# Loading the first two x tiles already transposed, and the KV transposes one Q unit later

## The chip, the cores and the metric

The kernel runs on one NeuronCore of one Trainium2 chip. The metric is the device time of one execution in microseconds (us). A profile records one execution; its span runs from the first to the last instruction that the profiler shows. Engines are named as in the profile: PE is TensorE's matmul, PEld its weight load, DVE is VectorE, ACT is ScalarE, POOL is GpSimd, SP is SyncE, which here issues DMAs only.

## The reference: what is computed

For x of 2048 tokens by 1024 features, in bf16:

```python
g = sigmoid((x * gate_w).sum(-1))
# A: linear attention, 32 heads of 32
q, k, v = split(x @ wqkv)
phi(t) = where(t > 0, t + 1, exp(t)) + 1e-6
kv = sum_s phi(k)^T v ;  z = sum_s phi(k)
o = (phi(q) @ kv) / (phi(q) @ z + 1e-6)
a = o @ wo
# B: one token, chosen by a router, goes through a gated FFN
r = x @ w_r ;  idx = argmax(r)
y = (silu(x[idx] @ w_gate) * (x[idx] @ w_up)) @ w_down
b = x ;  b[idx] += sigmoid(r[idx]) * y
out = g * a + (1 - g) * b
```

## The kernel before

The sequence is cut into 16 tiles of 128 tokens, the features into 8 chunks of 128. TensorE wants x with features on the partitions, so a transposed copy `xT` (128 x 8 chunks x 2048) is kept on chip. The work comes in three stages:

1. Keys and values. For each tile, `kv_mm` multiplies the tile of `xT` (as weights) with the key columns of wqkv, two halves of 512 columns, 8 chunks each; `unit_V` does the same for the value columns, and for the router's and gate's vectors, which stand in two further columns of `wkv`. ACT and DVE apply phi. `unit_KVACC` adds up phi(k)^T v and the sum of phi(k) of a tile in one bank, `kvacc`. The FFN of the one token is woven in on DVE and TensorE.
2. Queries. `unit_Q(g, j)` makes 128 query features for 512 tokens in 8 products (`ps` from `xT` and `wq`), and ACT and DVE turn them into `pq_all`. Most of them are woven into stage 1; the last ones come after it. Among these last ones stand the FFN's final sum (`down_finish`, tile `yps`), the denominators (`den_group`, tile `dps`), the transposition of kv (`unit_kvT`, tile `pt`, 32 products on tiles of 32 x 32 of the array), and the product of kv with wo (`unit_M`, tile `pm`), which reads `kvT`.
3. Output. For each tile, 16 products of `pq_all` with that merged matrix `m_sb`, then a mix with x by the gate, and a store.

The order on each engine is that of the program where the flag `strict` is set: the helper `in_order` (line 78) then chains each instruction of an engine behind the one before it. All of them are recorded under its line, 83, so groups are told apart by their tiles. Where `strict` is off, a scheduler orders by data dependence.

The start of the kernel matters here. TensorE begins with `N_WARM` = 6 products of constants (`warm`, lines 263 to 267, tile `warm_ps`). Meanwhile SP issues on its one queue, in this order (lines 136 to 150): x tile 0, key chunk 0 (`load_k(0)`, called k0 below), x tile 1, key chunks 1 to 7 (k1 to k7), the last 10 heads of the values (called v), then DMA transposes that write `xT` directly (tiles 2 and 3 one by one, then three groups of four tiles), the rest of the values, and `wq`. Tiles 0 and 1 come as they lie in memory (`xnat`); `unit_T` (line 200) transposes such a tile on TensorE, 8 blocks of 128 x 128 into two banks (`pst`), which DVE and ACT copy to `xT`. Then the first two tiles' key products run side by side, so that each chunk of the keys serves 4 products as it arrives: `first_mm(t, c0, c1)` (line 272) does 2 products of 512 columns per tile and chunk, into four banks called `first`. Tile 0's chunk c goes together with tile 1's chunk c - 1. The small product `wps` (line 281) puts the router's and gate's vectors into `wkv`.

PSUM has 8 banks: `ps_work` 4, `ps_ffn` 1, and 3 that are first `ps_t`, then `ps_acc` and `ps_red`, then `ps_den`.

The order at the end of the queries is given by these lines:

```python
    down_finish()
...
    rdA = den_group(0)
    strict[0] = True
    unit_kvT()
    strict[0] = False
    normalise(rdA, 0)
    normalise(rdA, 1)
    strict[0] = True
    for i in range(len(q_units)):
        unit_Q(*q_units.popleft())
        if i in M_AFTER:
            unit_M(*M_AFTER[i])
```

## Time and profile before

| what | us |
|---|---|
| three executions | 248.56, 248.9, 249.45 |
| median | 248.9 |
| the profiled execution | 248.56 |
| its span | 247.0 |
| PE busy | 240.8 (97% of the span) |
| DVE busy | 172.7 (70%) |
| ACT busy | 127.6 (52%) |
| POOL busy | 52.5 (21%) |
| TensorE clock granted, mean | 1.000 |

The profile has a page and a trace behind it. The chain that ended last is followed back from the last instruction: at each step to what released it, or to the instruction before it on its engine; in order of time it shows what the end of the kernel depended on. A timeline gives start, length, engine, line, operation, the tile written and the tile read; `x8` merges eight instructions. For a DMA two times are given: how long its issue kept SP (SPq), and how long it took from the start of its issue until its data had landed. A table by stretch gives, for stretches of the span, each engine's busy time, the granted clock, the share of the DMA engines' time in use, and what they moved in GB/s.

### The profile page before, as it was taken

Reading aid. Unit: us, or ns where it says so; the run is one execution under the profiler, and the core shown is the slowest. Engines: PE = TensorE matmul, PEld = TensorE weight load, DVE = VectorE, ACT = ScalarE, POOL = GpSimd, SP = SyncE. Lnnn points to the kernel's source line nnn. Section 1 sums busy time; section 2 is a strip of 40 time slices with the busy share of each in tenths; the row PEclk is TensorE's granted clock in tenths of the full one; section 3 lists DMA queues with packets and bytes.
Section 4 is the critical chain, followed back from the end, with each engine's and each line's share of the span. In section 5 each row is a group of like instructions: output and inputs, shape, how many; then the busy total and the mean of one; then the engine's idle time right before and its main releaser. Section 6 shows DMA issues by size and latency. Waiting matters only on the chain.

```text
span 247.0 us, 4867 instructions
## 1 busy us (share of the span) xinstructions
PE 240.8 (97%) x1898; PEld 123.6 (50%) x1923; DVE 172.7 (70%) x264; ACT 127.6 (52%) x215; POOL 52.5 (21%) x100
## 2 busy tenths in 40 slices
PE   8999999999999999999999999999999999999994
PEld 3466756654554554554554555544443444444442
DVE  0053124379984989845989999996789999954342
ACT  3195343355566376545555555668887633333300
POOL 6000000400000100000003300101666689950000
PEclk9999999999999999999999999999999999999999
DMA  6999995499969993599699690000004754464122
GB/s 207 343 239 195 267 392 151 108 326 337 281 194 292 341 290 88 149 312 384 224 345 340 230 280 3 3 4 21 0 3 127 204 182 148 155 190 166 48 82 86
DMA packets 46311, 47.78 MB, mean 193 GB/s; under 512 B 16776, under 2 KB 35472, under 8 KB 46224
## 3 DMA queue, kind: packets, MB, share of 16 engines
q1 hardware_dynamic: 45648, 46.28, 61.5%
q0 software_dynamic: 608, 1.19, 1.7%
q8 instruction: 15, 0.25, 0.5%
q14 instruction: 8, 0.07, 0.1%
q10 hardware_dynamic: 32, 0.00, 0.0%
HBM read 39.33 MB, written 8.39 MB: 193 GB/s over the span
## 4 chain that ended last, share of the span: by engine, by line
PE 97%; issue 1%; DVE 0%; DVEq 0%
PE ps L83 88%; PE first L83 3%; PE kvacc L83 2%; PE warm_ps L83 1%; PE red L83 1%; PE dps L83 1%; PE pst L83 1%; PE pm L83 1%; DVE ot L83 0%; PE yps L83 0%; PE pt L83 0%; DVEq L739 0%; PE hps L83 0%; PE rps L83 0%; PE wps L83 0%
## 5 line engine op out<-in xcount | busy, mean ns | idle before, releaser
L83 PE MATMUL ps<-wkv,xT 128*128 128x352 bf16 (+2 forms) x600 | 106.1, 334 | 0.4
L83 PEld LDWEIGHTS <-xT 128*128 128x128 bf16 x640 | 62.1, 98 | 49.1 <-issue 0.3
L83 ACT ACTIVATE u<-ps 128x512 f32<-128x512 f32 x60 | 35.9, 598 | 46.3 <-PE ps L83 45.7
L83 PE MATMUL ps<-xT,wq 128*128 128x512 bf16 x245 | 57.3, 379 | 0.6 <-issue 0.2
L83 PE MATMUL ps<-m_sb,pq_all 128*128 128x512 bf16 (+2 forms) x259 | 55.4, 373 | 0.3
L83 ACT ACTIVATE e<-u 128x512 f32<-128x512 f32 x64 | 40.3, 630 | 2.0
L83 PEld LDWEIGHTS <-pq_all 128*128 128x128 bf16 x264 | 25.4, 98 | 30.2 <-issue 0.7
L641 POOL TENSOR_TENSOR pq_all<-pq_all,rb 128x512 bf16<-128x512 bf16 x32 | 36.4, 1171 | 12.1 <-DVE rb L83 11.5
L83 PEld LDWEIGHTS <-wq 128*128 128x128 bf16 x256 | 24.5, 98 | 28.2 <-issue 1.0
L83 DVE SCALAR_TENSOR_TENSOR gacc<-wt,hcol,gacc 128x1024 f32<-128x1024 bf16 x27 | 34.5, 1278 | 0.4
L83 DVE SCALAR_TENSOR_TENSOR ot<-ps,gate,xg 128x512 bf16<-128x512 f32 (+2 forms) x33 | 23.9, 738 | 14.3 <-PE ps L83 13.1
L83 DVE SCALAR_TENSOR_TENSOR gacc<-wt,xs_f,gacc 128x2048 f32<-128x2048 bf16 x14 | 32.8, 2345 | 0.2
L83 ACT ACTIVATE xg<-xt,omg 128x1024 f32<-128x1024 bf16 x16 | 18.2, 1147 | 26.8 <-DVE ot L83 25.8
L83 DVE SCALAR_TENSOR_TENSOR pq_all<-ps,e 128x512 bf16<-128x512 f32 x32 | 21.9, 687 | 11.3 <-ACT e L83 11.3
L83 DVE SCALAR_TENSOR_TENSOR pk<-ps,e 128x512 bf16<-128x512 f32 x28 | 19.0, 686 | 11.8 <-ACT e L83 11.6
L83 DVE STREAM_SHUFFLE rb<-rdp 128x512 f32<-128x512 f32 x32 | 22.8, 753 | 0.0
L83 ACT CAST vt<-ps 128x352 bf16<-128x352 f32 x32 | 14.4, 453 | 11.4 <-PE ps L83 11.1
L214 POOL MEMSET vt<- 128x22 bf16 x16 | 3.7, 432 | 75.7 <-PE kvacc L83 75.2
L83 ACT CAST vc<-ps 128x320 bf16<-128x320 f32 x16 | 6.5, 428 | 7.3 <-PE ps L83 7.3
L83 DVE COPY rg<-ps 128x2 f32<-128x2 f32 x16 | 2.5, 159 | 10.2 <-ACT vc L83 10.1
L355 POOL DMA_DIRECT2D xs<-in_A_x_dram x1 | 0.7, 711 | 39.3 <-DVE sig L83 39.3
L83 DVE SCALAR_TENSOR_TENSOR pk<-first,e 128x512 bf16<-128x512 f32 x4 | 2.8, 692 | 7.9 <-ACT e L83 7.9
(100 smaller groups left out, 94.9 us busy)
## 6 DMA issues: line engine op xcount, KB each, us to landing
wt<-in_B_w_down_dram SPq DMA_DIRECT2D x14, 512.0 KB, 4.9
wt<-in_B_w_gate_dram SPq DMA_DIRECT2D x8, 512.0 KB, 7.6
wt<-in_B_w_up_dram SPq DMA_DIRECT2D x8, 512.0 KB, 8.3
xt<-xp SPq DMA_DIRECT2D x16, 256.0 KB, 2.7
out_dram<-ot SPq DMA_DIRECT2D x15, 256.0 KB, 2.0
wt<-in_B_w_gate_dram SPq DMA_DIRECT2D x8, 384.0 KB, 7.6
wt<-in_B_w_up_dram SPq DMA_DIRECT2D x8, 384.0 KB, 7.2
wkv<-in_A_wqkv_dram SPq DMA_DIRECT2D x8, 256.0 KB, 4.4
```

The lines of the kernel that those rows point to most:

```text
L83: inst = fn(*a, **k)
L214: nc.gpsimd.memset(vt_t[t][:, :, 32:33], 1.0)
L355: nc.gpsimd.dma_start(out=xs8[:], in_=x2d[bass.ds(idx_val, 1), :].rearrange("o (c p) -> (o c) p", p=P))
L641: nc.gpsimd.tensor_tensor(sl, sl, rb[:], op=ALU.mult)
```

## The change

Tiles 0 and 1 of x are no longer loaded as they lie and transposed on TensorE. SP issues a DMA transpose for each of them, at the places of the queue where the plain loads stood. `unit_T` and its calls go, with three short warm-up products; the long warm-ups become 8, and two short ones stand behind `wps`, which takes a bank of `ps_t` in place of that of `ps_ffn`. On the other side, `yps` takes the bank of `ps_ffn` and `dps` one of `ps_den` in place of banks of `ps_work`, and `unit_kvT` stands behind the first Q unit that follows the denominators, not in front of it.

```diff
-N_WARM = 6
+N_WARM = 8
...
-    def load_x(t0, n):
-        xt4 = xin.tile([P, n, D], BF, name=f"xnat{t0}", bufs=1)
-        sp.dma_start(out=xt4[:, 0:n, :], in_=x_v[:, t0 : t0 + n, :])
...
-    load_x(0, 1)
+    def load_xt(t):
+        sp.dma_start_transpose(out=xT[:, :, t * P : (t + 1) * P], in_=x2d[t * P : (t + 1) * P, :])
+
+    load_xt(0)
     load_k(0)
-    load_x(1, 1)
+    load_xt(1)
     for c in range(1, KC):
         load_k(c)
...
-    unit_T(0)
-    warm(3, 128)
     first_mm(0, 0, 1)
-    wps = ps_ffn.tile([P, 16], BF, tag="f")
+    wps = ps_t.tile([P, 16], BF, tag="t")
     pe.transpose(wps[:], wrg_rows[:], ident[0:16, 0:16])
     dve.tensor_copy(wkv[:, :, 2 * D : 2 * D + 2], wps[:].rearrange("p (w c) -> p c w", w=2))
-    unit_T(1)
+    warm(2, 128)
...
     def down_finish():
-        ps = ps_work.tile([P, 512], F32, tag="w", name="yps")[:, 0:256]
+        ps = ps_ffn.tile([P, 256], F32, tag="f", name="yps")
...
     def den_group(pair):
-        pool, tag = (ps_work, "w") if pair == 0 else (ps_den, "d")
-        dps = pool.tile([P, 512], F32, tag=tag, name="dps")
+        dps = ps_den.tile([P, 512], F32, tag="d")
...
     rdA = den_group(0)
-    strict[0] = True
-    unit_kvT()
-    strict[0] = False
...
     for i in range(len(q_units)):
         unit_Q(*q_units.popleft())
+        if i == 0:
+            unit_kvT()
         if i in M_AFTER:
             unit_M(*M_AFTER[i])
```

## The prediction

> **What bounds the kernel now.** I read the page's busy shares and its chain that ended last, then the same chain in order of time for the first 14 us, then the SP queue's issues one by one with their landings, then the DMA rate by stretch. The shares and the chain's summary on the page:

> ```profile
> PE 240.8 (97%) x1898; PEld 123.6 (50%) x1923; DVE 172.7 (70%) x264; ACT 127.6 (52%) x215; POOL 52.5 (21%) x100
> ...
> PE 97%; issue 1%; DVE 0%; DVEq 0%
> ```

> TensorE's work is the time: whatever delays it by 1 us costs 1 us, and removed work pays only where TensorE would otherwise have had data. The chain in order of time (start, length, what):

> ```profile
> 1.02 2.72 PE warm_ps L83 x6
> 3.74 1.02 PE pst L83 x8
> 4.76 0.32 PE warm_ps L83 x3
> 5.08 0.85 PE first L83 x2
> 5.93 0.12 PE wps L83
> 6.05 0.59 PE pst L83 x8
> 6.64 4.59 PE first L83 x21
> ...
> 162.25 0.31 PE pt L83 x32
> ```

> Two things are to be seen. The x transposes (pst, 1.02 and 0.59 us) stand before 6.64. And TensorE is slow at first: a 512-column product takes 0.85/2 = 0.43 us at 5.08 (a warm-up 2.72/6 = 0.45) and 4.59/21 = 0.22 from 6.64. So it ran at half speed until about 6.1 us, after some 5.1 us of unbroken work.

> What are the transposes in front of? Timeline of SP, and issues with landings (last number: us from issue to landing), asked for one at a time: the issue of key chunk 1 (k1), the first two DMA transposes, the landing of k1.

> ```profile
> 2.39 0.43 SPq L83 DMA_DIRECT2D wkv<-in_A_wqkv_dram  x1
> ```
> ```profile
> 6.51 4.36 SPq L83 DMA_TRANSPOSE xT<-in_A_x_dram  x1
> ```
> ```profile
> 10.92 1.75 SPq L83 DMA_TRANSPOSE xT<-in_A_x_dram  x1
> ```
> ```profile
> wkv<-in_A_wqkv_dram SPq DMA_DIRECT2D x1, 256.0 KB, 4.1
> ```

> k1 lands at 2.39 + 4.1 = 6.49, and the products that read it start at 6.64. From there TensorE needs 4 x 0.219 = 0.87 us per chunk and runs dense to 13.17; the last chunk, k7, issued at 5.24 with 5.7 to its landing, is there at 10.94 for a product at about 11.9. So the pst work lies almost wholly in the wait for k1: only 6.64 - 6.49 = 0.15 us of it is on the path. Later pieces of the same queue are as tight: the v part lands at 5.71 + 7.2 = 12.91 for 13.17, the first large transpose at 12.72 + 7.9 = 20.62 for a product at 20.98.

> DMA rate by stretch (last column GB/s; the first is the stretch in us):

> ```profile
> 2.70:6.50 3.80, 3.80 (x25) 2.01 (x24) 0.65 (x3) 1.07 (x2) 2.23 (x16) 1.00 0.98 334
> 6.50:11.20 4.70, 4.70 (x24) 2.11 (x23) 0.38 (x1) 0.58 (x1) 0.00 (x0) 1.00 1.05 359
> 12.00:12.75 0.75, 0.75 (x5) 0.32 (x4) 0.00 (x0) 0.60 (x1) 0.00 (x0) 1.00 1.00 111
> 12.75:14.00 1.25, 1.25 (x10) 0.82 (x9) 0.58 (x1) 1.21 (x3) 0.00 (x0) 1.00 1.28 288
> 14.00:15.20 1.20, 1.20 (x11) 0.85 (x10) 0.75 (x2) 1.17 (x3) 0.00 (x0) 1.00 0.81 126
> 27.75:29.00 1.25, 1.25 (x11) 0.90 (x10) 0.16 (x1) 0.58 (x2) 0.00 (x0) 1.00 0.99 80
> ```

> Copies run at 334 to 359, a transpose at best at 288. Where the queue passes from copies to transposes (12.00) it drops to 111, at the start of a large transpose (14.00) to 126, from transposes back to copies (27.75) to 80.

> **Part one: the x tiles.** *Removed:* 16 transposes (1.02 + 0.59 us of chain), 3 short warm-ups (0.32), two copies of 0.42 us on DVE and two of 0.59 on ACT. On the path they are worth 0.15 us, as above; next late is k1. *Added, hidden:* two warm-ups of 0.45, so the eight end at 1.02 + 8 x 0.453 = 4.64; the cover is the first product's wait for k0, which lands no earlier than its 4.24 of now (1.44 + 2.8). Without it they would cost 0.4. Two short warm-ups (0.21) lie in the wait for k1.

> *Moved:* SP issues transpose 0, k0, transpose 1, k1 to k7, v, then all it issued before. What stands behind the two transposes is every key chunk, the v part, transposes of tiles 2 to 15, and wq; TensorE waits for all of them in turn. An issue of x took 0.40 and 0.45 us. An issue of a transpose of the same 128 rows took 4.36 and 1.75. The 4.36 I read as a full queue: counting issued packets less those done in the trace, some 1,500 to 1,700 were outstanding at the end of every one of the five transposes' issues, long or short, so the issue waits for room; at 1 us the queue is empty. I therefore take the nearest row, 1.75, for both: k0 is issued at 0.98 + 1.75 + 0.05 = 2.78, and lands 2.8 later at 5.6; transpose 1 is issued at 3.2, k1 at 5.04 and lands, with x0's own 2.7 from issue to landing on a short queue, at 7.74. The chunk-1 products start there and not at 6.64: **+1.1 us**. Later pieces come at their old spacing behind k1, so they add nothing of their own.

> Bounds of this term by the stream. Rate alone: two times 0.262 MB at 288 in place of 345 GB/s is 0.15 us each, k1 at 6.79, +0.15. All switches charged: two passes from transpose to copy (1.25 us at 80 of 383 loses 0.99), one from copy to transpose (0.75 us at 111 of 288 loses 0.46), one slow start (1.2 us at 126 of 282 loses 0.66), and the rate: 3.4 us, k1 at 9.9, +3.25. The issue row lies between.

> [...]

> **The clock.** Now TensorE works without a gap from 1.02. After, it idles from 4.64 to 5.6 and, after two products, wps and two warm-ups (0.85 + 0.12 + 0.21), from 6.8 to 7.74. What such gaps do is not in the trace. At best nothing. At worst the 5.1 us of slow work start afresh with k1, and half of it is lost: 2.55. Before k1 there are 3.62 + 1.18 = 4.8 us of work, nearly the 5.1 that sufficed, so I take a value near the lower end: **+0.5**. [...]

> **Part two: kvT, yps, dps.** The same 32 + 8 + 16 products, other banks. kvT (pt, 0.31) moves behind one unit of 8 Q products. TensorE passes once more from small tiles to whole ones; after such a passage 32 products took 169.57 - 162.56 = 7.01 us, where 16 took 3.40 without, so one costs 0 to 7.01 - 6.80 = 0.21: **+0.1**. Waits it could add are covered: pt needs the dps bank back from ACT (0.69 us from 162.4) and the yps bank from DVE (0.48 from 161.7), both during that Q unit (1.73). DVE's kvT copies stand behind the 3.35 us reciprocal as now, and end near 167.4 for a first reader (pm) at 169.6; without that cover pm and all products behind it would slip one for one. Q units get their four banks back; no bank wait over 0.2 us stands in the chain there, so I book no gain.

> **Sum.** Against the profiled execution (248.56, span 247.0): 248.56 + 1.1 + 0.5 + 0.1 = 250.26. The median of the three runs, 248.9, is 0.34 above it; with that, **250.6**.

> **Rivals.** (a) *The transposes come like copies* (lower bounds; the queue is empty, and the 1.75 too was waiting for room): k1 by 6.8 to 7.3, clock as now, 248.56 + 0.15 to 0.75, with the 0.34 up to 249.6: no change. (b) *The switches and the clock*: for it, 80 GB/s for 1.25 us; against, that was before chunks of other shape. k1 at 8.5 to 9.9, and longer gaps leave the clock low: +1.9 to 3.25, +0.1, +0.6 to 2.55: 251.5 to 254.4. A one-time cost of the first transpose (4.36 - 1.75 = 2.6 us) would land here too. (c) *Faster*: the copies' slow beginning (193 GB/s from 2.0 to 2.7) is spared and k1 lands early. With 288 there, 0.45 us; with the 0.15 of removed transposes 0.6; it decides only if k1 lands before 5.9, and v and the large transpose (0.26 and 0.36 us of room) must come earlier too. 247.9 to 248.1. That the change does not do what it says cannot be: in the built order no x transpose is left on TensorE.

> **Numbers.** 0.3% (0.75 us) is about what a measurement can tell from no change. Forecast (249.65 to 251.5): 0.47; (a) 0.22; (b) 0.25; (c) 0.06. Faster 0.06, same 0.22, slower 0.72. Range from the lower bound, 248.7, to all upper bounds at once, 248.56 + 3.25 + 2.55 + 0.1 = 254.4.

> **What would show it.** Issue of the first transpose near 1.75 us (0.4: (a); over 4: one-time cost); k1 landed near 7.7 and the chunk-1 products starting there; those products 0.43 us long (clock) or 0.22; the products from 13 us on as dense as now; pt 8 products behind dps with no wait in front of pm. I am wrong if k1 lands by 6.8, or if the delay at the front is made up by a wait that vanishes later.

## The result and the profile after

The changed kernel takes **255.08 us** (median of 4 runs, 254.47 to 255.52) against 248.84 for the kernel before, measured beside it on the same chip (4 runs, 248.56 to 249.45): a ratio of 1.0246, 95% interval 1.0214 to 1.0277. The forecast of 250.6 had the direction and missed the size; its range ended at 254.4. The profiled execution took 255.52, with a span of 254.0, so it is 6.96 longer than the profiled one of before.

Busy shares and the chain's summary on the page of the changed kernel:

```profile
PE 242.5 (95%) x1884; PEld 123.1 (48%) x1908; DVE 171.9 (68%) x262; ACT 126.6 (50%) x213; POOL 52.6 (21%) x100
...
PE 94%; DMA 2%; SPq 1%; issue 1%; DVE 0%; DVEq 0%
```

TensorE is still the time, but with 15 products fewer it is busy 1.7 us longer, and the chain now holds DMA and SP's queue beside it. Where, the chain in order of time tells (start, length, what):

```profile
0.98 1.36 SPq L83
...
3.02 1.24 SPq L83
...
4.31 5.22 DMA wkv<-in_A_wqkv_dram
...
9.57 9.23 PE first L83 x30
...
90.42 0.32 PE ps L83
90.75 1.12 issue
91.86 9.68 PE ps L83 x49
...
169.12 1.83 PE ps L83 x8
170.95 0.22 PE pt L83 x32
```

Read from the top: SP issues transpose 0 (1.36 us), k0, transpose 1 (1.24 us), and k1 at 4.31, 1.92 later than before. k1 takes 5.22 to its landing, where it took 4.1. The products of chunk 1 start at 9.57 and not at 6.64: **+2.93**. The same 30 products then take 9.23; before, the stretch from 6.64 to 13.17 held them in 6.53: **+2.70**. At 90.75 TensorE stands still for 1.12 with no releaser that the profile shows; before, it was 0.05: **+1.07**. The two rows of before on which the second and third of these figures rest:

```profile
13.17 6.32 PE ps L83 x41
...
84.95 0.05 issue
```

At the end the order is as the diff has it, 8 products and then pt. These three make 6.70 of the 6.96; the last 0.26 are spread over small differences.

The 2.70 are the clock: the granted clock is half for the 5.29 us from 9.57 to 14.86, and half of that is 2.65. A table by stretch of the changed kernel, in steps of 3.41 us (busy time of the engines, then the granted clock, DMA share and GB/s):

```profile
1.20:4.62 3.42, 3.39 (x8) 1.01 (x7) 0.00 (x0) 1.28 (x1) 3.04 (x34) 1.00 0.63 120
4.62:8.03 3.41, 0.92 (x5) 0.36 (x5) 0.17 (x1) 0.00 (x0) 0.49 (x5) 1.00 1.09 270
8.03:11.45 3.42, 1.88 (x5) 0.69 (x5) 0.00 (x0) 0.00 (x0) 0.00 (x0) 0.50 0.94 317
11.45:14.86 3.41, 3.41 (x9) 1.18 (x8) 0.00 (x0) 0.00 (x0) 0.00 (x0) 0.50 1.33 293
14.86:18.27 3.41, 3.41 (x17) 1.53 (x16) 0.00 (x0) 0.51 (x1) 0.00 (x0) 1.00 1.02 230
```

In the first row the clock's 1.00 means only that no record is there yet: a warm-up takes 3.57/8 = 0.45 us in it, twice the 6.53/30 = 0.22 of a first product before, so it is half speed. The record opens at 4.62. In the next step TensorE is busy 0.92 of 3.41 us and the clock closes at 8.03. It stays at half through a step that is busy for 1.88, and opens again at 14.86, after one that is full. Nine products in 3.41 us, and then 17: that is where the 2.70 go. Of the other three executions, two were granted the same mean clock as this one, 0.986; the fourth was granted 0.999 and took 254.47 all the same. It has no trace, and a mean of 0.999 doesn't say that its first products ran at full speed: act_q2 below has 0.999 too, and its record opens only at 20.39.

### The profile page after: what moved, and what is told of

Its sections match the earlier page's. It is cut to its first block, busy times and chain, and to the rows that moved or that the text cites. A ratio compares the mean times of both kernels' runs of the same rounds, so it can differ in the third digit from the quotient of the medians.

```text
span 254.0 us, 4831 instructions
## 1 busy us (share of the span) xinstructions
PE 242.5 (95%) x1884; PEld 123.1 (48%) x1908; DVE 171.9 (68%) x262; ACT 126.6 (50%) x213; POOL 52.6 (21%) x100
## 4 chain that ended last, share of the span: by engine, by line
PE 94%; DMA 2%; SPq 1%; issue 1%; DVE 0%; DVEq 0%
PE ps L83 85%; PE first L83 4%; DMA wkv<-in_A_wqkv_dram 2%; PE kvacc L83 2%; SPq L83 1%; PE red L83 1%; PE dps L83 1%; PE pm L83 1%; DVE ot L83 0%; PE yps L83 0%; DVEq L723 0%; PE pt L83 0%; PE hps L83 0%; PE rps L83 0%; PE xs_ps L83 0%
## 5 line engine op out<-in xcount | busy, mean ns | idle before, releaser
L83 PE MATMUL ps<-wkv,xT 128*128 128x352 bf16 (+2 forms) x600 | 106.1, 334 | 0.4
L83 PEld LDWEIGHTS <-xT 128*128 128x128 bf16 x640 | 62.8, 99 | 56.0 <-issue 8.0
L83 ACT ACTIVATE u<-ps 128x512 f32<-128x512 f32 x60 | 35.9, 598 | 47.6 <-PE ps L83 47.4
L83 PE MATMUL ps<-xT,wq 128*128 128x512 bf16 x246 | 57.6, 379 | 1.8 <-issue 1.4
L83 PE MATMUL ps<-m_sb,pq_all 128*128 128x512 bf16 (+2 forms) x258 | 55.1, 372 | 0.4 <-issue 0.2
L83 ACT ACTIVATE e<-u 128x512 f32<-128x512 f32 x64 | 40.3, 630 | 2.0
L83 PEld LDWEIGHTS <-pq_all 128*128 128x128 bf16 x264 | 25.4, 98 | 30.2 <-issue 0.7
L626 POOL TENSOR_TENSOR pq_all<-pq_all,rb 128x512 bf16<-128x512 bf16 x32 | 36.5, 1162 | 12.1 <-DVE rb L83 11.5
L83 PEld LDWEIGHTS <-wq 128*128 128x128 bf16 x256 | 24.3, 98 | 29.5 <-issue 2.8
L83 DVE SCALAR_TENSOR_TENSOR gacc<-wt,hcol,gacc 128x1024 f32<-128x1024 bf16 x27 | 34.5, 1279 | 0.4
L83 DVE SCALAR_TENSOR_TENSOR ot<-ps,gate,xg 128x512 bf16<-128x512 f32 (+2 forms) x33 | 23.9, 735 | 14.3 <-PE ps L83 14.2
L83 DVE SCALAR_TENSOR_TENSOR gacc<-wt,xs_f,gacc 128x2048 f32<-128x2048 bf16 x14 | 32.8, 2346 | 0.2
L83 ACT ACTIVATE xg<-xt,omg 128x1024 f32<-128x1024 bf16 x16 | 18.1, 1147 | 26.9 <-DVE ot L83 25.9
L83 DVE SCALAR_TENSOR_TENSOR pq_all<-ps,e 128x512 bf16<-128x512 f32 x32 | 21.9, 686 | 11.5 <-ACT e L83 11.5
L83 DVE SCALAR_TENSOR_TENSOR pk<-ps,e 128x512 bf16<-128x512 f32 x28 | 19.0, 686 | 12.7 <-ACT e L83 12.7
L83 DVE STREAM_SHUFFLE rb<-rdp 128x512 f32<-128x512 f32 x32 | 22.7, 748 | 0.0
L83 ACT CAST vt<-ps 128x352 bf16<-128x352 f32 x32 | 14.5, 453 | 12.8 <-PE ps L83 12.8
L83 PE MATMUL first<-wkv,xT 128*128 128x512 bf16 x32 | 9.8, 475 | 4.1 <-DMA wkv<-in_A_wqkv_dram 4.1
L83 DVE SCALAR_TENSOR_TENSOR pk<-first,e 128x512 bf16<-128x512 f32 x4 | 2.8, 692 | 13.5 <-ACT e L83 13.5
L83 ACT CAST vc<-ps 128x320 bf16<-128x320 f32 x16 | 6.5, 428 | 7.3 <-PE ps L83 7.3
## 6 DMA issues: line engine op xcount, KB each, us to landing
xt<-xp SPq DMA_DIRECT2D x16, 256.0 KB, 2.6
out_dram<-ot SPq DMA_DIRECT2D x15, 256.0 KB, 2.0
wkv<-in_A_wqkv_dram SPq DMA_DIRECT2D x8, 256.0 KB, 5.3
```

The lines of the kernel that those rows point to most:

```text
L83: inst = fn(*a, **k)
L626: nc.gpsimd.tensor_tensor(sl, sl, rb[:], op=ALU.mult)
```

## The experiments

Fourteen kernels were run, with the kernel before beside each group (medians 249.0 to 249.23).

**The two parts by themselves.** `p1_only` has the two DMA transposes, with yps, dps and pt as before. `p2_only` is the kernel before with yps, dps and pt as changed.

```diff
# p1_only, against the changed kernel
-        ps = ps_ffn.tile([P, 256], F32, tag="f", name="yps")
+        ps = ps_work.tile([P, 512], F32, tag="w", name="yps")[:, 0:256]
...
     rdA = den_group(0)
+    strict[0] = True
+    unit_kvT()
+    strict[0] = False
...
-        if i == 0:
-            unit_kvT()
```

> The x tiles by DMA alone; kvT, yps and dps as in the kernel before. Theory A (the front: key chunk 1 lands 3 us late, and the TensorE clock falls back to half because of the gaps, 2.65 us): nearly the whole loss is here, 254.0 to 255.5 us, chunk 1 landing near 9 us and a stretch of clock 0.5 from about 8 to 15 us. Rival B (part two costs the 1.3 us of the chain's delay that arises after 23 us): 253.5 to 254.0, and the chain's delay against the kernel before stays at about 5.6 us to the end.

> Part two alone: kvT behind the first Q unit, yps and dps in their other banks; x tiles as in the kernel before. Theory A: no difference, 248.5 to 249.5, within 0.3% of the kernel before. Rival B: 249.9 to 250.2, with a wait of TensorE of about 1 us between 80 and 190 us that the kernel before lacks.

Measured: p1_only 254.11 (253.56 to 254.72), ratio 1.0200 (1.0177 to 1.0223). p2_only 249.11 (248.71 to 249.56), ratio 1.0004 (0.9995 to 1.0014). The chain of p2_only around pt:

```profile
162.60 1.83 PE ps L83 x8
164.43 0.22 PE pt L83 x32
164.66 0.16 issue
```

Eight products, pt, and 0.16 us later the next product: part two costs nothing and brings nothing. The front is the cause. The 0.97 us between the medians of p1_only and the full change are not shown to be part two's own: in the profile of p1_only the wait near 90 us is 0.28 and not 1.12, which makes 0.84 of them.

**Is it the late issue, or the transposes that stand ahead?** `late_k` is the kernel before, with no DMA transpose ahead of the keys; k1 and all behind it on SP's queue are held until GpSimd has done a memset near 4 us.

```diff
# late_k, against the kernel before
-    for c in range(1, KC):
-        load_k(c)
...
     c4_set = nc.gpsimd.memset(c4[:], 0.0)
+    k1_ld = load_k(1)
+    tc.add_manual_dep(k1_ld.ins, c4_set.ins.name, SYNC, reason="late issue")
+    for c in range(2, KC):
+        load_k(c)
...
```

> The kernel before (tiles 0 and 1 loaded as they lie and transposed on TensorE, no DMA transpose ahead of the keys); the only change is that k1's issue waits for GpSimd's memset of c4, near 4.1 us, so that k1 and everything behind it on SP's queue is issued about as late as in the changed kernel (4.31 there, 2.39 in the kernel before). It tells the lateness of the issue from what a DMA transpose does to the copies behind it. Theory (the issue is 1.9 us of the loss, and the transposes ahead of k1 are the further 1.1 us in its landing): k1 lands 2.7 to 3.2 us after its issue, by 6.8 to 7.3, chunk 1 starts there, 0.3 to 0.7 us later than 6.64, the clock stays open, 249.2 to 249.9 us against 249.0. Rival (a copy issued at 4.3 takes its 4 to 5 us whatever stands ahead of it, since the queue's transfers come only later): k1 lands at 8.1 to 9.4, the gap on TensorE is as long as in the changed kernel, 250.5 to 252.

Measured: 250.02 (249.44 to 251.6), ratio 1.0037 (1.0017 to 1.0057). k1 is issued at 4.04; the issue, with its time to landing:

```profile
wkv<-in_A_wqkv_dram SPq DMA_DIRECT2D x1, 256.0 KB, 2.7
```

It lands at 6.73 and chunk 1 starts at 6.77, 0.13 later than before. An issue 1.65 us late is therefore worth 0.13 there, no more than two profiles of the same front differ by (p2_only starts chunk 1 at 6.88). Issued at 4.31 as in the changed kernel and landing in the same 2.7, k1 would be there at an estimated 7.0, 0.5 later than before. The rest of its lateness, 2.5 us here and 1.5 to 2.5 in the six profiles with this queue order, comes with the transposes ahead of k1. What the lateness does cost comes behind: the chain of late_k waits for the v part.

```profile
7.26 7.00 DMA wkv<-in_A_wqkv_dram
...
14.31 6.48 PE ps L83 x41
```

v lands at 14.26 in place of 12.95, and the products that want it start 1.14 us later than before; late_k's median is 0.83 above that of the kernel before. In the changed kernel v lands later still, at 15.49, but the slow products want it only at 18.80.

**The clock, with the gaps filled one by one.** In the changed kernel TensorE has two gaps, 4.59 to 5.99 (waiting for k0) and 6.9 to 9.57 (for k1). `fill1` fills the first with warm-ups, `fill2` the second, `fill` both.

```diff
# fill and fill1
-N_WARM = 8
+N_WARM = 14
# fill and fill2
-    warm(2, 128)
+    warm(12)
```

> The changed kernel with constant products in TensorE's two waits: 14 long warm-ups in place of 8 ahead of the first products, 12 long ones in place of 2 short ones behind wps. They compute nothing that is used. Theory A: the clock opens near 4.6 us and stays at 1.0, products of chunk 1 take 0.22 us from the start: 2.65 us less than the changed kernel, 252.0 to 252.8; chunk 1 still lands near 9 us. Rival C (the clock falls for another reason than the gaps, such as the missing transposes): 254.5 to 255.5 with clock 0.5 from 8 us on.

> The changed kernel with constant products in the first of TensorE's two waits alone (14 long warm-ups in place of 8; nothing more behind wps). Theory C1 (any long gap within a clock window of 3.4 us closes the clock, so the second gap of over 2 us does it alone): clock 0.5 returns at about 8 to 12 us and lasts at least 3.4 us, 253.5 to 255.0. Rival C2 (the two gaps are needed together): no stretch of 0.5 after the opening, 251.0 to 252.0.

> The changed kernel with eight warm-ups as it has them, so that the first gap on TensorE (4.6 to 6.0) stays, and 12 long warm-ups behind wps in place of two short ones, so that the second gap (6.9 to 9.6) is filled. With fill (both filled: clock open from 5.75 on, 251.55) and fill1 (only the first filled: the clock stayed open, 251.73) it is the missing fourth case. Theory (both gaps together close the clock): it stays open as soon as it has opened, first products 6.5 us for the run as in fill, 251.3 to 252. Rival (the first gap alone closes it or delays its opening): the granted clock is half for 3.4 us or more after 8, the first run takes 8 us or more, 253 to 254.5.

| kernel | us | first product of chunk 1 | its 30 products | clock |
|---|---|---|---|---|
| changed | 255.08 | 9.57 | 9.23 us | opens 4.62, closes 8.03, opens 14.86 |
| fill | 251.55 (251.09 to 251.95) | 9.80 | 6.47 | opens 5.75, stays |
| fill1 | 251.73 (251.15 to 252.31) | 8.51 | 6.63 | opens 5.03, stays |
| fill2 | 252.41 (251.51 to 254.58) | 9.47 | 6.48 | opens 5.03, stays |

(The times of chunk 1 and the clock are those of one profiled execution each; that of fill2 took 251.51, and what the clock did in its longer runs isn't known.) The rows of the chain for fill (the run of first products, and what follows it):

```profile
9.80 4.53 PE first L83 x21
...
16.27 6.32 PE ps L83 x41
```

In these profiles the clock stays open with either gap filled and closes with both unfilled: neither gap closes it alone there. For the first gap that rests on one execution; two of fill2's four, at 253.29 and 254.58, took 1.8 and 3.1 us longer than it. The step after the opening in fill1 holds a wait of 1.57 us and stays open at 1.91 us of work:

```profile
5.03:8.44 3.41, 1.91 (x10) 0.75 (x9) 0.17 (x1) 0.00 (x0) 0.09 (x1) 1.00 1.02 245
```

Filling takes away 2.7 to 3.5 us by the medians, but not all of that is the clock: in the profiles of fill and fill2 the wait near 90 us is gone too, 1.07 us of it, and the clock's part is the 9.23 - 6.47 = 2.76 of the first products. The rest of the loss stays since k1 is still late: 8.46 to 8.86 in these three profiles. In fill and fill2 the 12 idle products also run past its landing, to 9.80 and 9.47, and in fill1 the products next wait for v, which lands at 15.28.

**Other orders on the queue.** `tt_first` issues both transposes ahead of all keys. `kk_first` issues k0 and k1 ahead of both transposes; `kk_fill` is that with 12 warm-ups. `x1_dma` transposes tile 0 on TensorE as before and only tile 1 by DMA, with part two undone.

```diff
# tt_first
     load_xt(0)
-    load_k(0)
     load_xt(1)
-    for c in range(1, KC):
+    for c in range(KC):
# kk_first; kk_fill has N_WARM = 12 too
-    load_xt(0)
     load_k(0)
+    load_k(1)
+    load_xt(0)
     load_xt(1)
-    for c in range(1, KC):
+    for c in range(2, KC):
# x1_dma, against the kernel before
-    load_x(1, 1)
+    sp.dma_start_transpose(out=xT[:, :, P : 2 * P], in_=x2d[P : 2 * P, :])
...
-    unit_T(1)
```

> The changed kernel with both DMA transposes issued ahead of all key chunks: one passage from transposes to copies in place of two. Theory A1 (each passage between a transpose and a copy costs the queue 0.3 to 1 us and leaves stragglers): chunk 0 lands at 6.3 to 6.8, chunk 1 at 7.2 to 8.0 in place of 9.5; 1.5 to 2.3 us faster than the changed kernel, 252.8 to 253.6, the clock still falling. Rival A2 (the lateness is the issue time of the two transposes alone, 1.36 + 1.24 us, and the slow first transposes): chunk 1 lands as late as in the changed kernel, 8.8 to 9.6, and the time is 254.5 to 255.5.

> The changed kernel with key chunks 0 and 1 issued ahead of the two DMA transposes, chunk 2 behind them. Theory A: the first products now wait for tile 0's transpose at 5.5 to 6.5 us, four to six products can run, then chunk 2 is the late one, at 9 to 10 us; the loss only moves by one chunk: 253.5 to 255.0. Rival A4 (what counts is chunk 1's own place behind transposes): 251 to 252.5.

> kk_first (k0 and k1 issued ahead of the two DMA transposes) with 12 warm-ups in place of 8, so that TensorE's first gap is closed and the clock opens before chunk 1. Theory (in kk_first the half clock from 7.49 to 10.06 cost half of it, 1.3 us, and the later arrival of chunk 1 0.85): the run of first products takes 6.5 us from 7.5 on and ends near 14.0, 250.3 to 250.9 against 251.87 for kk_first: the best that DMA transposes of both tiles give here, and still not below the kernel before. Rival (the copies and not the clock limit the run, k2 to k7 arriving late): 251.5 to 252.

> The kernel before with tile 1 alone by DMA transpose (at its old place, between key chunks 0 and 1), tile 0 still on TensorE. Theory A (one transpose in front of chunk 1 costs 1.24 us of issue less 0.45, and one passage from transpose to copy): chunk 1 lands at 7.6 to 8.6, the clock, with the shorter gaps, stays open: 249.8 to 251.2. Rival D (the first transpose of all is the costly one, by a one-time cost): nearly the whole loss stays with one transpose, 253 us or more.

Measured: tt_first 253.67 (253.16 to 254.86), ratio 1.0203; kk_first 251.87 (251.13 to 252.31), 1.0115; kk_fill 251.17 (250.53 to 252.69), 1.0066; x1_dma 250.86 (249.66 to 252.79), 1.0077. In tt_first k0 lands only at 7.80, and the clock is at half from 8.73 to 12.14. In kk_first chunk 1 starts at 7.49, yet the clock first opens at 10.06, and 0.5 x (10.06 - 7.49) = 1.3 us are lost to it. kk_fill opens it at 6.13, and gains only 0.7 of these 1.3: in its profiled execution (252.69, the longest of four) the chain waits for a key chunk instead.

```profile
6.20 5.84 DMA wkv<-in_A_wqkv_dram
...
12.08 4.04 PE first L83 x18
```

The chunk issued at 6.20 landed at 12.04; 15 of its 16 parts were there at 10.15, and one 2 KB packet took 2,207 ns, from 8.97 on. Such late packets are not the transposes' alone: the kernel before has one of 1,093 ns among its first copies and p2_only one of 1,382. The two 2 KB packets over 2 us stand in kernels with transposes ahead; that the transposes make them isn't shown. With one transpose in place of two (x1_dma), k1 is issued at 3.30 and lands at 7.12, 3.8 later, and tile 0's own transposes keep TensorE at work; the clock opens at 6.14 and stays. With the small variant of it below (249.69), it comes nearest to the kernel before.

**The transposes on another queue.** `act_q` has ACT issue the two transposes; SP's queue then begins with k0 and k1. There the small loads of the router's and gate's rows (wrg_rows) stood behind the transposes, landed at 10.32 and held wps and all of TensorE behind it until 10.46, so its 255.43 (255.06 to 256.76) tell nothing of the question. `act_q2` puts these loads first.

```diff
# act_q and act_q2
-        sp.dma_start_transpose(out=xT[:, :, t * P : (t + 1) * P], in_=x2d[t * P : (t + 1) * P, :])
+        nc.scalar.dma_start_transpose(out=xT[:, :, t * P : (t + 1) * P], in_=x2d[t * P : (t + 1) * P, :])
# act_q2: moved ahead of them
+    nc.scalar.dma_start(out=wrg_rows[0:8, :], in_=B_w_r.rearrange("(c p) -> c p", p=P))
+    nc.scalar.dma_start(out=wrg_rows[8:16, :], in_=gate_w.rearrange("(c p) -> c p", p=P))
```

> The changed kernel with the two DMA transposes issued by ACT, in front of its own two small loads, and the key chunks by SP at once. Theory A1 (the issue time of the two transposes, 2.6 us ahead of chunk 1 on SP, is the larger part of its lateness): chunk 1 lands before 8.0 us, 1.5 to 3 us faster than the changed kernel. Rival A3 (the transposes themselves on the DMA engines, at half the rate of copies at the start, and packets that lag behind them, are the larger part): the first products wait for tile 0 instead, chunk 1 or tile 0's transpose lands at 8 us or later, less than 1 us faster.

> The changed kernel with the two first DMA transposes issued by ACT, behind the small loads of the router's and gate's rows (which stand behind them in act_q, where they were late and held TensorE). SP's queue then begins with k0 and k1. Theory (the issue on SP delays k1 by 1.9 us, and the transposes slow whatever runs beside them): k1 is issued near 1.5 to 2.5 and lands by 7, tile 0 lands at 5 to 6 as it runs beside the copies, first products near 6, chunk 1 from 7 to 7.5, clock at half speed for the first 3 to 4 us of it as in kk_first (one long gap ahead of it), 251 to 252.5. Rival (the transposes' own traffic is what delays k1, by whichever queue they come): k1 lands at 8.5 or later, 253 to 255.

act_q2 measured 261.53 (260.9 to 261.99), ratio 1.0490 (1.0464 to 1.0516): both theories fell, and by far. k1 landed early, at 4.44; what came late were the two transposes, at 12.94 and 16.20, and the key chunks from k3 (11.44) on. Its two transposes, with the median time to landing, and what was moved from 4.5 to 11.5 us, in the row by stretch:

```profile
xT<-in_A_x_dram ACTq DMA_TRANSPOSE x2, 12.0
```
```profile
4.50:11.50 7.00, 0.09 (x1) 0.00 (x0) 0.00 (x0) 1.28 (x1) 0.61 (x5) 1.00 1.22 143
```

In the same stretch the kernel before moved 354 GB/s:

```profile
4.50:11.50 7.00, 6.95 (x40) 3.31 (x39) 0.89 (x3) 1.17 (x2) 0.61 (x5) 1.00 1.04 354
```

In act_q2, with the transposes on one queue beside the copies of another, both crawl at 143 GB/s together. Moving the issue away from SP didn't help, and here transposes next to copies were dearer than ahead of them. No run has transposes on ACT's queue without copies beside them, so that ACT's queue itself is slow for them isn't excluded.

**The wait near 90 us.** No step of the prediction has it. In the profiles up to here it stands, with 0.28 to 1.36 us, in all eight kernels with 1,908 to 1,914 weight loads on TensorE, and in none of the six with 1,915 to 1,924. `fill1_w15` steps over that bound from fill1 (0.94 us of wait) by one product, `x1_w2` from x1_dma (no wait) the other way.

```diff
# fill1_w15, against fill1
-N_WARM = 14
+N_WARM = 15
# x1_w2, against x1_dma
-    warm(3, 128)
+    warm(2, 128)
```

> fill1 with one product more: 15 long warm-ups in place of 14, so 1,915 weight loads on TensorE in place of 1,914. In the profiles so far a wait of 0.3 to 1.4 us on TensorE at 87 to 96 us, which the profile puts down to no releaser, stands in all eight kernels with 1,908 to 1,914 weight loads (fill1: 0.94) and in none of the six with 1,915 to 1,924. Theory (the wait depends on the number of instructions on TensorE and not on how late the front is): the wait is gone, the front as in fill1 or up to 0.25 us later, 250.6 to 251.1 us against 251.73. Rival (it depends on how late TensorE arrives there, or on chance): the wait of about 0.9 stays, 251.6 to 252.1.

> x1_dma with one product less: two short warm-ups ahead of the first product in place of three, so 1,914 weight loads in place of 1,915; TensorE waits for k1 after that in any case. Theory of the count: the wait near 86 us, absent in x1_dma, appears with 0.3 to 1.1 us, 251.1 to 252 us against 250.86. Rival (lateness or chance, not the count): no wait, 250.6 to 251.1.

Measured: fill1_w15 251.28 (250.75 to 251.75), ratio 1.0079; x1_w2 249.69 (249.36 to 252.53), ratio 1.0033 (1.0001 to 1.0065). In fill1 and in fill1_w15 the chain near 87 us reads:

```profile
87.14 0.94 issue
```
```profile
87.72 0.05 issue
```

One product more and the wait is gone. But x1_w2, with 1,914 weight loads, has no wait either, so the count alone does not set it: the theory of the count fell on one of its two tests. In each profile that has the wait it ends 1.2 to 1.5 us after a 16 KB packet of the queue that the profile names "instruction" has landed; in the changed kernel that packet is under way from 89.46 to 90.61. In the eight profiles with the wait the packet lands 0.1 to 1.1 us ahead of the place where TensorE then stops. In the eight without it, fill1_w15 and x1_w2 among them, it lands 1.9 to 3.8 us ahead of that place (in the kernel before at 81.18 for 84.95). That TensorE waited there for its own instructions is argued from this and not shown; what sets when they are fetched stays open.

No kernel of the fourteen is below the kernel before.

## Why the prediction was wrong, step by step

**What bounds the kernel, and where the change is felt: right.** TensorE, the wait for k1, and first products at half speed if the gaps close the clock. Part one is 5.1 of the 6.2 us (p1_only), and p2_only shows nothing of the other 1.1 in part two alone; the removed products brought nothing.

Two terms of the sum were mis-sized, the landing of k1 (+1.1, measured +2.93) and the clock (+0.5, measured +2.70), and a third cost, 1.07 us, was in no term.

**"k1 at 5.04 and lands, with x0's own 2.7 from issue to landing on a short queue, at 7.74 ... +1.1": the mechanism right, the price wrong.** The issue was taken too dear: 1.36 and 1.24 us where 1.75 was booked (4.36 does not recur at the head of the queue, which fits the full queue that was argued), so k1 is issued at 4.31. The landing was taken too cheap. The 2.7 hold for a copy on a short queue with no transpose ahead, as x0 and late_k's k1 show. Behind two transposes k1 took 4.2 to 5.2 in the six profiles that have the changed kernel's queue order. Transpose 1 lands at 6.94, where x1's plain copy landed at 5.68; k1 comes 2.59 after it, where it came 0.81 after x1. In the changed kernel 15 of k1's 16 parts were there at 8.11, and the last came at 9.53; one 2 KB packet that started at 6.59 took 2,029 ns, where the median is 84. About 1.4 of the 2.93 is that last part; over the six profiles k1 landed at 8.46 to 9.53, 2.0 to 3.0 later than before, so +1.1 was too low in all. The bound from the switches (k1 at 9.9) was near the upper end, though it had no late packet in it. The choice between the bounds was the error: I took the row of the issue as the nearest, while the rows that showed what happens between a transpose and a copy, 80 GB/s for 1.25 us, stood in the same table. They were set aside since the chunks there had another shape. Why copies come later behind a transpose stays open.

**"Nearly the 5.1 that sufficed, so I take a value near the lower end: +0.5": wrong, +2.70.** The step asked how much work had been done before k1. Work done did not keep the clock open: it had opened at 4.62, after 3.6 us of work, and closed again at 8.03. That 5.1 us were needed before was chance: the clock opened at 6.09, the end of one of its steps (last section). The step also took 2.55 as the worst, on the thought that a slow phase lasts 5.1 us; here it lasted 6.83, of which 5.29 fell on work. Rival (b), "longer gaps leave the clock low", describes what happened; it had 0.25.

**"Part two ... +0.1": right within its bounds**, 0.0 by p2_only. Its covers held: no wait in front of pm.

**"Later pieces come at their old spacing behind k1": right.** From k1 to v it is 15.49 - 9.53 = 5.96 us, and was 6.46. This hides a floor that the sum did not name: had the clock stayed open, v would have been the next to be late, as in fill1 (15.28) and late_k (14.26), where the products wait for it.

**Missing: 1.07 us** of the wait near 90 us. With it, the landing near its upper bound of 3.25 and the clock just over its 2.55 went past the range, 255.1 against 254.4; without it they would have stayed inside. The range's upper end was also added up from the profiled 248.56, while the forecast has the 0.34 up to the median in it; with that and part two's own upper bound of 0.21 it is 254.9, still short of 255.1. In rival (c) the 0.45 doesn't follow from its row: 193 in place of 288 GB/s for 0.7 us is 0.23. Nothing else rests on it.

## What to carry to other kernels

When copies stand behind a DMA transpose in one queue, price the passage by what the trace shows of such a passage (here 0.9 to 1.8 us more than behind a copy, in each profile another value). Moving the transposes to a second queue beside the copies was the dearest order here (act_q2, 261.53 us). Where a change opens gaps on TensorE near the start, lay them over the clock's steps of 3.41 us, from several starting points: here the clock closed after a step that was 27% busy, and then products took twice their time until a step had been full. Filling both gaps with idle products did not shorten the wait for k1 here (chunk 1 starts at 9.80, and at 9.57 without), yet it saved 3.5 of 6.2 us, 2.76 of them by the clock.

## What the runs showed that was not expected

```profile
1.90:5.31 3.41, 2.69 (x7) 0.79 (x6) 0.00 (x0) 1.28 (x1) 2.86 (x28) 1.00 0.86 158
```
```profile
13.56:16.97 3.41, 2.49 (x9) 0.72 (x8) 0.17 (x1) 0.00 (x0) 0.00 (x0) 1.00 1.06 295
```
```profile
5.89:9.31 3.42, 1.68 (x9) 0.86 (x9) 0.17 (x1) 0.00 (x0) 0.00 (x0) 1.00 0.97 305
```

If other executions keep to these bounds, the changed kernel's gaps cost, wherever the clock is closed at 9.57, an estimated 1.3 to 2.9 us: half of the time from 9.57 to the end of the first step that is some three quarters busy (at the earliest one that begins at 8.7 and ends at 12.1; at the latest one that begins at 12.0 and ends at 15.4). On steps that are busy for 27 to 49% the profiles say nothing, so a starting point at which the clock stays open isn't excluded.

**Transposes at the head of an empty queue.** In the changed kernel the DMA transposes of 128 rows keep SP for 1.36 us on the empty queue and for 1.24 behind transpose 0 and k0, three times a copy's 0.40. The first packet of transpose 0 comes at 2.40, and its 0.26 MB are done at 3.99: 165 GB/s, where the best stretch of the kernel before showed 288 for one in full flow.
